# Gate operands turned channel-major by DMA transposes, and a second buffer for the output tile

## The chip, the core and the metric

The kernel runs on one core of one Trainium2 chip. The metric is the device time of one execution in microseconds (us); a kernel's figure is the median of its runs. The engines are named as the profile names them: PE (TensorE matmul) and PEld (its weight loads), DVE (VectorE), ACT (ScalarE), POOL (GpSimd), and SP (SyncE), which here only issues DMAs. A trailing q (SPq) is an engine's instruction queue.

## The reference

A gated linear recurrence runs along 5824 positions of 4 sequences, on 256 channels, and its output goes through a multiplicative feed-forward block.

```python
sig_r = 1.0 / (1.0 + np.exp(-r_gate))
sig_i = 1.0 / (1.0 + np.exp(-i_gate))
log_a = c * sig_r * np.log(np.clip(a_base, 1e-06, 1.0 - 1e-06))[None, None, :]   # c = 8
a_t = np.exp(log_a)
norm = np.sqrt(np.maximum(1.0 - a_t * a_t, 1e-06))
x_gated = norm * sig_i * x
for t in range(S):
    h = a_t[:, t] * h + x_gated[:, t]
    y[:, t] = h
...
a = x @ w1          # x: y as 23296 x 256
b = x @ w2          # w1, w2: 256 x 1024
h = a * b @ w3      # w3: 1024 x 1024
return (h @ w_out).astype(np.float32)   # w_out: 1024 x 256
```

## The kernel before

The 23296 tokens are cut into 46 chunks, the first of 256 tokens and the others of 512. Inputs arrive token-major (128 tokens on the partitions, 256 channels in the row). The recurrence needs channels on the partitions, so that DVE's scan can run along the tokens; two operands have to be turned on the way.

For a chunk c the work is this. `load` fetches r, i and x (three DMAs of 512 KB from SP). `tanh_r` and `tanh_i` take the two tanh on ACT (a sigmoid is half of a tanh plus a half), and POOL makes u = sigmoid(i) times x. `tr_r` turns tanh(r) with 8 PE transposes of 128x128 into a PSUM tile `ptr`; `decay` is the exp on ACT that reads `ptr` and writes a. `square` on POOL and `root` on ACT make the norm; `tr_u` turns u into `ptr` too, and `gated` on DVE multiplies norm and u. `scan` (two per chunk) and `cast` on DVE end the recurrence. The feed-forward part takes four quarters per chunk: `up` makes `pa` and `pb` on PE (4 matmuls each), ACT copies `pa` to `sa`, DVE multiplies `sa` and `pb` into `g`; `down` multiplies 128 tokens of g with a weight into `po`. That weight is w3 times w_out, made on the chip once by `fold`. `store` copies half a chunk of `po` (256 tokens) to `ot`, on ACT for the first half and on DVE for the second, and SP writes it out.

PSUM is full: `pa` and `pb` share a pool of three tiles of two banks, `ptr` has one bank (pool `psum_t`), and `po` has one (pool `psum_o`). So the second half's `down` cannot start before the first half's copy has ended, and tr_r and tr_u of all chunks go through one tile.

The order is written out by hand: every engine executes its instructions in the order in which the loop issues them. A step s has four quarters. In step s, PE does `up` of chunk s and `down` of chunk s-2; DVE does gated, scan, scan and cast of chunk s+2, one in each quarter. The gate work of tanh, transposes, exp, square and root is queued in groups of chunks (1, 1, 2, 3, then 4 each), spread over the quarters of the steps before the group's first `gated`, by weights written beside each operation; within a group all roots come last, since tanh and sqrt need different tables on ACT. `load` of a chunk is issued six quarters ahead of its tanh_r. Three buffers each hold r, i, x and `ot`.

Of the kernel before, what the change touches and what calls it, by code (L numbers as in the profile page):

```python
# [18 lines left out]
def kernel(  # L19
# [45 lines left out]
    psum = ctx.enter_context(tc.tile_pool(name="psum", bufs=3, space=bass.MemoryType.PSUM))  # L65
    psum_t = ctx.enter_context(tc.tile_pool(name="psum_t", bufs=1, space=bass.MemoryType.PSUM))
    psum_o = ctx.enter_context(tc.tile_pool(name="psum_o", bufs=1, space=bass.MemoryType.PSUM))

# [24 lines left out]
    def tanh_r(c):  # L93
        n = sizes[c] // P
        t = gates.tile([P, 4, D], BF16, name="th_r", tag="th_r")
        nc.scalar.activation(out=t[:, :n, :], in_=T["r", c][:, :n, :], func=AF.Tanh, scale=0.5)  # L96
        T["thr", c] = t

    def tanh_i(c):
        n = sizes[c] // P  # L100
        t = gates.tile([P, 4, D], F32, name="th_i", tag="th_i")
        nc.scalar.activation(out=t[:, :n, :], in_=T["i", c][:, :n, :], func=AF.Tanh, scale=0.5)  # L102
        u = held.tile([P, 4, D], BF16, name="u_t", tag="u")
        nc.gpsimd.tensor_scalar(t[:, :n, :], t[:, :n, :], 1.0, 0.5, op0=ALU.add, op1=ALU.mult)  # L104
        nc.gpsimd.tensor_mul(out=u[:, :n, :], in0=t[:, :n, :], in1=T["x", c][:, :n, :])  # L105
        T["u", c] = u

    def transposes(src, n):
        pt = psum_t.tile([P, NCB, CT], BF16, name="ptr", tag="ptr")
        for cb in range(NCB):  # L110
            for j in range(n):
                nc.tensor.matmul(  # L112
                    out=pt[:, cb, j * P:(j + 1) * P],
                    lhsT=src[:, j, cb * P:(cb + 1) * P], rhs=ident,
                    is_transpose=True,
                    start=(cb == 0 and j == 0), stop=(cb == NCB - 1 and j == n - 1))
        return pt

    def tr_r(c):
        T["pr", c] = transposes(T["thr", c], sizes[c] // P)  # L120
        T["a", c] = held.tile([P, NCB, CT], F32, name="a_t", tag="a")

# [16 lines left out]
    def tr_u(c):  # L139
        T["pu", c] = transposes(T["u", c], sizes[c] // P)  # L140

# [70 lines left out]
    def fold(mi):  # L212
        w3 = ffn.tile([P, DFF], BF16, name="w3_t", tag="w3")
        nc.gpsimd.dma_start(out=w3, in_=moe_w3[mi * P:(mi + 1) * P, :])
        pt = psum_t.tile([P, KD, P], BF16, name="ptw", tag="ptr")
        for k in range(KD):
# [15 lines left out]
    for k, g in enumerate(groups):  # L232
        last = g[0] - LEAD - 1
        first = groups[k - 1][0] - LEAD if k else last
        ops = []
        for c in g:
            ops.append((1.04, lambda c=c: tanh_r(c)))
            ops.append((1.04, lambda c=c: tanh_i(c)))
            ops.append((0.7, lambda c=c: (tr_r(c), decay(c, 0))))
            ops.append((0.7, lambda c=c: (decay(c, 1), square(c))))  # L240
        for c in g:
            ops.append((1.05, lambda c=c: root(c)))
        total = sum(d for d, _ in ops)
        npos = 4 * (last - first + 1)
        acc = 0.0
        for n_op, (d, fn) in enumerate(ops):
            pos = min(npos - 1, int(npos * (acc + d / 2) / total))
            queue.setdefault((first + pos // 4, pos % 4), []).append(fn)
            if n_op < 4 * len(g) and n_op % 4 == 0:
                tanh_at[g[n_op // 4]] = 4 * first + pos  # L250
            acc += d
# [21 lines left out]
    for s in range(s0, NCH + LAG):  # L273
        for mp in range(4):
# [56 lines left out]
```

## Time and profile before

| | us |
|---|---|
| median of 3 runs | 681.7 (680.56 to 685.91) |
| the profiled execution's own time | 687.18 |
| its span in the trace | 685.4 |
| PE busy | 555.9 (81% of the span) |
| DVE busy | 492.2 (72%) |
| ACT busy | 440.6 (64%) |
| POOL busy | 274.1 (40%) |
| granted TensorE clock, mean | 0.974 of full speed |

The stages differ, so the shares of the whole span say little. Until about 99 us the first chunks go through the gate work, the weights arrive and are folded; from there to about 607 us all parts run side by side, in a pattern that repeats every four steps; then the gate work is done, from about 651 us the recurrence too, and only `up` and `down` are left. The profile is read stage by stage: first the stretches, then who waits for whom in one stretch, then single quarters in order of time.

### The profile page before, as it was taken

Reading aid. Unit: us, or ns where it says so; the run is one execution under the profiler, and the core shown is the slowest. Engines: PE = TensorE matmul, PEld = TensorE weight load, DVE = VectorE, ACT = ScalarE, POOL = GpSimd, SP = SyncE. Lnnn points to the kernel's source line nnn. Section 1 sums busy time; section 2 is a strip of 40 time slices with the busy share of each in tenths; the row PEclk is TensorE's granted clock in tenths of the full one; section 3 lists DMA queues with packets and bytes.
Section 4 is the critical chain, followed back from the end, with each engine's and each line's share of the span. In section 5 each row is a group of like instructions: output and inputs, shape, how many; then the busy total and the mean of one; then the engine's idle time right before and its main releaser. Section 6 shows DMA issues by size and latency. Waiting matters only on the chain.

```text
span 685.4 us, 9681 instructions
## 1 busy us (share of the span) xinstructions
PE 555.9 (81%) x3784; PEld 346.3 (51%) x3784; DVE 492.2 (72%) x438; ACT 440.6 (64%) x492; POOL 274.1 (40%) x155
## 2 busy tenths in 40 slices
PE   0326478788897898898887898898898898899995
PEld 0224344455564455555554555555555555556564
DVE  1316269678787788788787788788688688898851
ACT  6734068586785687687685677687687686574441
POOL 3663238626514516516515435435435433330000
PEclk9999599899999999999998999999999999999999
DMA  9993524282482365355355167168068055111112
GB/s 205 352 249 98 123 62 142 90 270 85 137 260 95 123 198 171 121 188 183 121 176 180 44 194 254 36 195 261 32 189 273 32 178 188 35 47 47 47 62 77
DMA packets 99901, 99.71 MB, mean 145 GB/s; under 512 B 4112, under 2 KB 98320, under 8 KB 99856
## 3 DMA queue, kind: packets, MB, share of 16 engines
q1 hardware_dynamic: 97120, 95.44, 43.7%
q0 software_dynamic: 2736, 3.67, 3.2%
q8 instruction: 29, 0.48, 0.3%
q14 instruction: 16, 0.13, 0.1%
HBM read 78.91 MB, written 23.86 MB: 150 GB/s over the span
## 4 chain that ended last, share of the span: by engine, by line
PE 35%; DVE 23%; issue 18%; ACT 14%; DMA 6%; POOL 3%; SPq 1%; DVEq 0%; ACTq 0%; POOLq 0%
PE po L197 14%; PE pa L178 8%; DVE g_t L190 7%; PE pb L186 7%; ACT sa L181 7%; DVE h_t L164 5%; DMA i_t<-in_i_gate_dram 5%; DVE y_t L170 4%; DVE ot L207 4%; PE ptr L112 4%; PE pw L223 2%; ACT a_t L125 2%; DVE nrm L144 2%; ACT th_i L102 2%; POOL nrm L131 1%
## 5 line engine op out<-in xcount | busy, mean ns | idle before, releaser
L190 DVE TENSOR_TENSOR g_t<-sa,pb 128x1024 bf16<-128x1024 bf16 (+1 forms) x184 | 220.9, 1200 | 111.5 <-ACT sa L181 100.9
L181 ACT CAST sa<-pa 128x1024 bf16<-128x1024 f32 (+1 forms) x184 | 184.2, 1001 | 118.6 <-PE pa L178 116.5
L197 PE MATMUL po<-wp_sb,g_t 128*128 128x256 bf16 x1456 | 189.3, 274 | 53.2 <-DVE ot L207 51.5
L197 PEld LDWEIGHTS <-g_t 128*128 128x128 bf16 x1456 | 142.7, 98 | 115.2 <-issue 66.1
L186 PE MATMUL pb<-y_t,w_sb 128*128 128x512 bf16 (+1 forms) x736 | 190.3, 382 | 2.9 <-ACT sa L181 2.9
L178 PE MATMUL pa<-y_t,w_sb 128*128 128x512 bf16 (+1 forms) x736 | 191.6, 384 | 0.2 <-DVE g_t L190 0.2
L104 POOL TENSOR_SCALAR th_i<-th_i 128x1024 f32<-128x1024 f32 (+1 forms) x46 | 50.7, 1102 | 241.4 <-ACT th_i L102 151.8
L164 DVE TENSOR_TENSOR_SCAN h_t<-a_t,h_t,nrm 128x512 f32<-128x512 f32 (+3 forms) x90 | 137.2, 1526 | 0.0
L131 POOL TENSOR_TENSOR nrm<-a_t 128x1024 f32<-128x1024 f32 (+1 forms) x46 | 99.1, 2153 | 79.8 <-ACT a_t L125 79.8
L105 POOL TENSOR_TENSOR u_t<-th_i,x_t 128x1024 bf16<-128x1024 f32 (+1 forms) x46 | 117.8, 2562 | 5.9 <-DMA x_t<-in_x_dram 2.1
L186 PEld LDWEIGHTS <-w_sb 128*128 128x128 bf16 x736 | 73.1, 99 | 92.0 <-issue 8.9
L125 ACT ACTIVATE a_t<-ptr,la 128x512 f32<-128x512 bf16 (+1 forms) x92 | 66.7, 772 | 68.4 <-PE ptr L112 68.4
L178 PEld LDWEIGHTS <-w_sb 128*128 128x128 bf16 x736 | 69.9, 99 | 47.5 <-issue 2.7
L144 DVE SCALAR_TENSOR_TENSOR nrm<-nrm,ptr 128x1024 f32<-128x1024 f32 (+1 forms) x46 | 55.6, 1209 | 38.2 <-PE ptr L112 20.3
L136 ACT ACTIVATE nrm<-nrm 128x1024 f32<-128x1024 f32 (+1 forms) x46 | 48.1, 1051 | 9.5 <-POOL nrm L131 9.4
L112 PE MATMUL ptr<-ident,th_r 128*128 128x128 bf16 x364 | 29.7, 228 | 29.8 <-ACT th_r L96 17.7
L170 DVE CAST y_t<-h_t 128x1024 bf16<-128x1024 f32 (+1 forms) x46 | 51.7, 1123 | 0.1
L205 ACT COPY ot<-po 128x512 f32<-128x512 f32 x46 | 27.0, 586 | 37.5 <-PE po L197 37.5
L102 ACT ACTIVATE th_i<-i_t 128x1024 f32<-128x1024 f32 (+1 forms) x46 | 48.4, 1052 | 2.5 <-DMA i_t<-in_i_gate_dram 2.5
L96 ACT ACTIVATE th_r<-r_t 128x1024 bf16<-128x1024 f32 (+1 forms) x46 | 48.7, 1059 | 0.2
L112 PEld LDWEIGHTS <-th_r 128*128 128x128 bf16 x364 | 25.0, 102 | 33.4 <-ACT th_r L96 19.8
L112 PE MATMUL ptr<-ident,u_t 128*128 128x128 bf16 x364 | 30.6, 232 | 11.1 <-POOL u_t L105 10.2
(28 smaller groups left out, 153.0 us busy)
## 6 DMA issues: line engine op xcount, KB each, us to landing
out_dram<-ot SPq DMA_DIRECT2D x91, 256.0 KB, 2.2
r_t<-in_r_gate_dram SPq DMA_DIRECT2D x45, 512.0 KB, 4.5
i_t<-in_i_gate_dram SPq DMA_DIRECT2D x45, 512.0 KB, 5.5
x_t<-in_x_dram SPq DMA_DIRECT2D x45, 512.0 KB, 5.8
w_t<-in_moe_w_dram POOLq DMA_DIRECT2D x8, 256.0 KB, 5.8
w_sb<-in_moe_w_dram POOLq DMA_DIRECT2D x2, 512.0 KB, 8.0
wo_sb<-in_moe_w_out_dram POOLq DMA_DIRECT2D x1, 512.0 KB, 14.3
r_t<-in_r_gate_dram SPq DMA_DIRECT2D x1, 256.0 KB, 2.9
```

Of the source, the lines that this page charges most:

```text
L105: nc.gpsimd.tensor_mul(out=u[:, :n, :], in0=t[:, :n, :], in1=T["x", c][:, :n, :])
L112: nc.tensor.matmul(out=pt[:, cb, j * P:(j + 1) * P], lhsT=src[:, j, cb * P:(cb + 1) * P], rhs=ident, is_transpose=True, start=(cb == 0 and ...
L125: nc.scalar.activation(out=T["a", c][:, cb, :w], in_=T["pr", c][:, cb, :w], func=AF.Exp, scale=la4[:, cb:cb + 1], bias=la4[:, cb:cb + 1])
L131: nc.gpsimd.tensor_mul(out=t[:, :, :w], in0=T["a", c][:, :, :w], in1=T["a", c][:, :, :w])
L144: nc.vector.scalar_tensor_tensor(out=T["n", c][:, :, :w], in0=T["n", c][:, :, :w], scalar=1e-3, in1=T["pu", c][:, :, :w], op0=ALU.max, op1 ...
L164: nc.vector.tensor_tensor_scan(T["h", c][:, cb, lo:hi], T["a", c][:, cb, lo:hi], T["n", c][:, cb, lo:hi], init, ALU.mult, ALU.add)
L170: nc.vector.tensor_copy(out=T["y", c][:, :, :w], in_=T["h", c][:, :, :w])
L178: nc.tensor.matmul(out=pa[:, q, :w], lhsT=w1_sb[:, cb, m * P:(m + 1) * P], rhs=T["y", c][:, cb, :w], start=(cb == 0), stop=(cb == NCB - 1))
L181: nc.scalar.copy(out=sa[:, :, :w], in_=pa[:, :, :w])
L186: nc.tensor.matmul(out=pb[:, q, :w], lhsT=w2_sb[:, cb, m * P:(m + 1) * P], rhs=T["y", c][:, cb, :w], start=(cb == 0), stop=(cb == NCB - 1))
L190: nc.vector.tensor_mul(out=T["g", c][:, 2 * mp:2 * mp + 2, :w], in0=sa[:, :, :w], in1=pb[:, :, :w])
L197: nc.tensor.matmul(out=T["po", c][:, j % 2, :], lhsT=T["g", c][:, k, j * P:(j + 1) * P], rhs=wp_sb[:, k, :], start=(k == 0), stop=(k == KD ...
```

## The change

The pool `psum_t` and the PE transposes are gone; `psum_o` gets two buffers, and the fold's transposes, which used the bank of `ptr`, now use `psum_o` too. tanh(r) and u are written by ACT and POOL with the two halves of the channels apart, each as four blocks of 128x128. A DMA transpose issued from SP turns all eight blocks in one instruction and writes a tile in SBUF (`rt` for tanh(r), `ut` for u); chunk 0 takes two DMAs for each. `decay` and `gated` read these tiles where they read `ptr`. The `rt` DMA is issued right after tanh_r. The exp of a chunk comes after the two tanh of the next chunk of its group, and `tr_u`, now a DMA, moves from the quarter of `gated` to the place just ahead of the exp. The moment of a load still is six quarters ahead of its tanh_r.

```diff
-    psum_t = ctx.enter_context(tc.tile_pool(name="psum_t", bufs=1, space=bass.MemoryType.PSUM))
-    psum_o = ctx.enter_context(tc.tile_pool(name="psum_o", bufs=1, space=bass.MemoryType.PSUM))
+    psum_o = ctx.enter_context(tc.tile_pool(name="psum_o", bufs=2, space=bass.MemoryType.PSUM))
...
     def tanh_r(c):
         n = sizes[c] // P
-        t = gates.tile([P, 4, D], BF16, name="th_r", tag="th_r")
-        nc.scalar.activation(out=t[:, :n, :], in_=T["r", c][:, :n, :], func=AF.Tanh, scale=0.5)
-        T["thr", c] = t
+        t = gates.tile([P, NCB, 4, P], BF16, name="th_r", tag="th_r")
+        nc.scalar.activation(out=t[:, :, :n, :].rearrange("p cb j q -> p j cb q"),
+                             in_=T["r", c][:, :n, :].rearrange("p j (cb q) -> p j cb q", q=P),
+                             func=AF.Tanh, scale=0.5)
+        T["pr", c] = turn(t, n, "rt")
+        T["a", c] = held.tile([P, NCB, CT], F32, name="a_t", tag="a")
...
-        u = held.tile([P, 4, D], BF16, name="u_t", tag="u")
+        u = gates.tile([P, NCB, 4, P], BF16, name="u_t", tag="u")
...
-        nc.gpsimd.tensor_mul(out=u[:, :n, :], in0=t[:, :n, :], in1=T["x", c][:, :n, :])
+        nc.gpsimd.tensor_mul(out=u[:, :, :n, :].rearrange("p cb j q -> p j cb q"),
+                             in0=t[:, :n, :].rearrange("p j (cb q) -> p j cb q", q=P),
+                             in1=T["x", c][:, :n, :].rearrange("p j (cb q) -> p j cb q", q=P))
...
+    def turn(src, n, tag):
+        dst = (gates if tag == "rt" else held).tile([P, NCB, 4, P], BF16, name=tag, tag=tag)
+        if n == 4:
+            nc.sync.dma_start_transpose(out=dst.rearrange("p cb j q -> p (cb j) q"),
+                                        in_=src.rearrange("p cb j q -> p (cb j q)"))
+        else:
+            for cb in range(NCB):
+                nc.sync.dma_start_transpose(out=dst[:, cb, :n, :],
+                                            in_=src[:, cb, :n, :].rearrange("p j q -> p (j q)"))
+        return dst.rearrange("p cb j q -> p cb (j q)")
...
-        T["pu", c] = transposes(T["u", c], sizes[c] // P)
+        T["pu", c] = turn(T["u", c], sizes[c] // P, "ut")
...
-        for c in g:
-            ops.append((1.04, lambda c=c: tanh_r(c)))
-            ops.append((1.04, lambda c=c: tanh_i(c)))
-            ops.append((0.7, lambda c=c: (tr_r(c), decay(c, 0))))
-            ops.append((0.7, lambda c=c: (decay(c, 1), square(c))))
+        for c in g + [None]:
+            if c is not None:
+                ops.append((1.04, lambda c=c: tanh_r(c)))
+                ops.append((1.04, lambda c=c: tanh_i(c)))
+            if c != g[0]:
+                d = g[-1] if c is None else c - 1
+                ops.append((0.7, lambda d=d: (tr_u(d), decay(d, 0))))
+                ops.append((0.7, lambda d=d: (decay(d, 1), square(d))))
...
                 if mp == 0:
-                    tr_u(c)
                     gated(c)
```

How instructions stand now, at three places. First SP in the running stage, where a row is one DMA (r_t, i_t and x_t are loads, ot the output). Before:

```order
L209 DMA out_0_dram<-ot_2507 128x2x256
L88 DMA r_t_2541<-in_r_gate_dram 128x4x256
L88 DMA i_t_2543<-in_i_gate_dram 128x4x256
L88 DMA x_t_2545<-in_x_dram 128x4x256
L209 DMA out_0_dram<-ot_2583 128x2x256
```

and after:

```order
L115 DMA_TRANSPOSE rt_993<-th_r_991 128x8x128
L209 DMA out_0_dram<-ot_1017 128x2x256
L115 DMA_TRANSPOSE rt_1051<-th_r_1049 128x8x128
L87 DMA r_t_1054<-in_r_gate_dram 128x4x256
L87 DMA i_t_1056<-in_i_gate_dram 128x4x256
L87 DMA x_t_1058<-in_x_dram 128x4x256
L115 DMA_TRANSPOSE ut_1087<-u_t_1023 128x8x128
L209 DMA out_0_dram<-ot_1090 128x2x256
```

Two transposes per chunk have come in between the loads and the stores; each waits on SP for the ACT or POOL instruction that writes its source, and the rows below it wait with it.

Second, ACT in the running stage: from a chunk's tanh_r to its exp (`a_t`). `sa` is the copy of `pa`, one in each quarter. Before:

```order
L96 ACTIVATE th_r_1315<-r_t_1107 128x1024
L181 CAST sa_1322<-pa_1317 128x1024
L102 ACTIVATE th_i_1339<-i_t_1109 128x1024
L181 CAST sa_1352<-pa_1347 128x1024
L125 ACTIVATE a_t_1391<-ptr_1382,la4_89 128x512 x2
```

and after, for the chunk whose turned tile is rt_993:

```order
L95 ACTIVATE th_r_991<-r_t_802 128x4x2x128
L181 CAST sa_1001<-pa_996 128x1024
L205 COPY ot_1017<-po_979 128x512
L104 ACTIVATE th_i_1021<-i_t_804 128x1024
L181 CAST sa_1031<-pa_1026 128x1024
L95 ACTIVATE th_r_1049<-r_t_876 128x4x2x128
L181 CAST sa_1065<-pa_1060 128x1024
L104 ACTIVATE th_i_1082<-i_t_878 128x1024
L125 ACTIVATE a_t_995<-rt_993,la4_86 128x512
L181 CAST sa_1098<-pa_1093 128x1024
```

The exp has moved behind the next chunk's two tanh: three copies of `pa` stand between tanh_r and exp where there were two.

Third, SP at the start, from the load of chunk 2 (r_t_112 before, r_t_109 after). Before, the next rows are the loads of chunk 3:

```order
L88 DMA r_t_112<-in_r_gate_dram 128x4x256
L88 DMA i_t_114<-in_i_gate_dram 128x4x256
L88 DMA x_t_116<-in_x_dram 128x4x256
L88 DMA r_t_140<-in_r_gate_dram 128x4x256
L88 DMA i_t_142<-in_i_gate_dram 128x4x256
```

and after:

```order
L87 DMA r_t_109<-in_r_gate_dram 128x4x256
L87 DMA i_t_111<-in_i_gate_dram 128x4x256
L87 DMA x_t_113<-in_x_dram 128x4x256
L119 DMA_TRANSPOSE rt_121<-th_r_119 128x2x128 x2
L119 DMA_TRANSPOSE ut_130<-u_t_127 128x2x128 x2
L87 DMA r_t_138<-in_r_gate_dram 128x4x256
L87 DMA i_t_140<-in_i_gate_dram 128x4x256
L87 DMA x_t_142<-in_x_dram 128x4x256
L115 DMA_TRANSPOSE rt_149<-th_r_147 128x8x128
L115 DMA_TRANSPOSE ut_159<-u_t_155 128x8x128
```

Chunk 0's transposes stand behind the loads of chunks 0, 1 and 2, and chunk 1's behind those of chunk 3.

## Rows read from the trace of the kernel before

**Rows 1.** Page, engines: busy us, share of the span, instructions.
```profile
PE 555.9 (81%) x3784; PEld 346.3 (51%) x3784; DVE 492.2 (72%) x438; ACT 440.6 (64%) x492; POOL 274.1 (40%) x155
```

**Rows 2.** Stretches of the span, busy us (instructions), clock, DMA share, GB/s.
```profile
core 0: us, PE busy (x) PEld busy (x) DVE busy (x) ACT busy (x) POOL busy (x), PEclk, DMA share, GB/s
0.00:32.00 32.00, 5.00 (x39) 3.69 (x40) 7.89 (x11) 21.83 (x25) 14.46 (x17) 1.00 1.04 273
...
279.03:330.92 51.89, 45.97 (x320) 28.65 (x320) 42.05 (x37) 37.72 (x42) 23.57 (x13) 1.00 0.50 163
330.92:387.35 56.43, 48.80 (x320) 29.78 (x320) 43.81 (x38) 37.71 (x42) 23.05 (x13) 0.94 0.46 150
```

**Rows 3.** PE in order of time, one batch each: start us, us.
```profile
99.28 1.04 PE L197 MATMUL po<-wp_sb,g_t 128*128 128x256 bf16 x8
...
606.80 1.03 PE L197 MATMUL po<-wp_sb,g_t 128*128 128x256 bf16 x8 [1.05 <-DVE ot L207]
...
640.98 0.61 PE L112 MATMUL ptr<-ident,u_t 128*128 128x128 bf16 x8
641.42 1.03 PE L178 MATMUL pa<-y_t,w_sb 128*128 128x512 bf16 x4
...
653.80 1.04 PE L197 MATMUL po<-wp_sb,g_t 128*128 128x256 bf16 x8
...
656.40 1.04 PE L197 MATMUL po<-wp_sb,g_t 128*128 128x256 bf16 x8
```

**Rows 4.** Groups of 99.28 to 606.8 us: busy, mean ns, idle before.
```profile
L197 PE MATMUL po<-wp_sb,g_t 128*128 128x256 bf16 x1200 | 156.8, 274 | 48.4 <-DVE ot L207 48.4
```

**Rows 5.** Waits of 279 to 331 us: total us, times, longest.
```profile
DVE g_t L190 <- ACT sa L181: 8.1, 8, 3.1
...
ACT a_t L125 <- PE ptr L112: 5.9, 3, 4.1
...
PE po L197 <- DVE ot L207: 4.6, 4, 1.7
...
PE ptr L112 <- DVE nrm L144: 1.3, 1, 1.3
```

**Rows 6.** Groups of 279.03 to 330.92 us: busy, mean ns, idle before.
```profile
L190 DVE TENSOR_TENSOR g_t<-sa,pb 128x1024 bf16<-128x1024 bf16 x16 | 19.4, 1210 | 8.1 <-ACT sa L181 8.1
...
L144 DVE SCALAR_TENSOR_TENSOR nrm<-nrm,ptr 128x1024 f32<-128x1024 f32 x5 | 6.1, 1222 | 2.2 <-PE ptr L112 2.2
```

**Rows 7.** Page, DMA: packets, MB, share; issues: KB each, us to landing.
```profile
q1 hardware_dynamic: 97120, 95.44, 43.7%
...
out_dram<-ot SPq DMA_DIRECT2D x91, 256.0 KB, 2.2
...
x_t<-in_x_dram SPq DMA_DIRECT2D x45, 512.0 KB, 5.8
```

**Rows 8.** All engines in order of time, start of the span.
```profile
9.00 1.00 ACT L125 ACTIVATE a_t<-ptr,la 128x256 f32<-128x256 bf16 x2
...
11.95 3.90 SPq L88 DMA_DIRECT2D x_t<-in_x_dram  x1
...
16.16 1.06 ACT L96 ACTIVATE th_r<-r_t 128x1024 bf16<-128x1024 f32 x1
...
17.82 1.06 ACT L102 ACTIVATE th_i<-i_t 128x1024 f32<-128x1024 f32 x1 [0.60 <-DMA i_t<-in_i_gate_dram]
...
30.04 2.66 POOL L105 TENSOR_TENSOR u_t<-th_i,x_t 128x1024 bf16<-128x1024 f32 x1
...
39.88 1.06 ACT L136 ACTIVATE nrm<-nrm 128x1024 f32<-128x1024 f32 x1 [3.68 <-POOL nrm L131]
40.84 0.57 ACT L181 CAST sa<-pa 128x512 bf16<-128x512 f32 x1
```

**Rows 9.** The wait list of SP's own queue, whole span.
```profile
SPq L209 <- DVE ot L207: 243.3, 45, 8.0
...
SPq L88 <- POOL u_t L105: 44.4, 14, 3.8
```

More of the change, by code (lines that the diff above doesn't have):

```diff
@@ L102, in tanh_i @@
         nc.scalar.activation(out=t[:, :n, :], in_=T["i", c][:, :n, :], func=AF.Tanh, scale=0.5)
-        u = held.tile([P, 4, D], BF16, name="u_t", tag="u")
+        u = gates.tile([P, NCB, 4, P], BF16, name="u_t", tag="u")
         nc.gpsimd.tensor_scalar(t[:, :n, :], t[:, :n, :], 1.0, 0.5, op0=ALU.add, op1=ALU.mult)
-        nc.gpsimd.tensor_mul(out=u[:, :n, :], in0=t[:, :n, :], in1=T["x", c][:, :n, :])
+        nc.gpsimd.tensor_mul(out=u[:, :, :n, :].rearrange("p cb j q -> p j cb q"),
+                             in0=t[:, :n, :].rearrange("p j (cb q) -> p j cb q", q=P),
+                             in1=T["x", c][:, :n, :].rearrange("p j (cb q) -> p j cb q", q=P))
         T["u", c] = u
[L108 to L121, printed above, removed]
+    def turn(src, n, tag):
[8 more added lines that the diff above has]
+        return dst.rearrange("p cb j q -> p cb (j q)")
     def decay(c, cb):
@@ L214, in fold @@
         nc.gpsimd.dma_start(out=w3, in_=moe_w3[mi * P:(mi + 1) * P, :])
-        pt = psum_t.tile([P, KD, P], BF16, name="ptw", tag="ptr")
+        pt = psum_o.tile([P, KD, P], BF16, name="ptw", tag="po")
         for k in range(KD):
@@ L248 @@
             queue.setdefault((first + pos // 4, pos % 4), []).append(fn)
-            if n_op < 4 * len(g) and n_op % 4 == 0:
-                tanh_at[g[n_op // 4]] = 4 * first + pos
+            if n_op == 0:
+                tanh_at[g[0]] = 4 * first + pos
+            elif n_op < 4 * len(g) - 2 and n_op % 4 == 2:
+                tanh_at[g[n_op // 4 + 1]] = 4 * first + pos
             acc += d
```

## The prediction

> **What bounds the kernel now.** I start with the busy times [rows 1] and keep only that PE is the fullest engine and DVE the next: the span has stages, so I go on by stretches [rows 2]. The stretch from 279.03 to 330.92 us is four steps of the running stage; it repeats, but for three disturbed places such as the next stretch of 56.43 us. In it PE is busy 45.97 of 51.89 us at full clock, DVE 42.05, ACT 37.72, POOL 23.57, and the DMA engines 0.50. So no transfer limits it, and a step takes 12.97 us.
>
> How long the stage is comes from PE in order of time [rows 3]: the first `down` is at 99.28 us, and the one at 606.80 us is the last that I count. Between them are 1200 `down` matmuls [rows 4], 16 of chunk 0 and 37 times 32, so 38 steps in 507.5 us, 13.36 each with the disturbed places in.
>
> What a step could take shows at the end, where only `up` and `down` are left: one `down` starts 2.60 us after the other (653.80, 656.40), [rows 3], so four quarters are 10.4 us and four steps 41.6. The running stage takes 10.3 us more per four steps. Eight batches of PE transposes explain 3.5 to 4.9 of them (a batch occupies PE for 0.44 us, 640.98 to 641.42, or 0.61 by its duration, [rows 3]); PE's wait for the DVE copy of `ot`, which is the wait for the one `po` tile, 4.6; and PE's wait for the one `ptr` tile 1.3 [rows 5]. These add up to 9.4 to 10.8: PE, with its waits, is the bound, and the change takes away all three.
>
> **The change, part by part.**
>
> *PE.* 728 transposes and as many weight loads go. `down` of the second half no longer waits for the first half's copy. PE would then need 41.6 us per four steps.
>
> *What is next.* DVE is busy 42.05 us in the same four steps [rows 2], just above PE's 41.6. DVE now also idles 8.1 us for `sa` [rows 5, 6]. Part of this is PE being late with `pa`, and part is ACT being held 5.9 us by exps that wait for PE's `ptr` [rows 5]. If all of it goes, a step is 42.05 / 4 = 10.5 us; if all stays, (42.05 + 8.1) / 4 = 12.5 us. Both causes are hit, but three engines with 42, 42 and 38 us of work in fixed order will still trip over each other, so I take the middle, 11.5 us. The gain is 38 x (13.36 - 11.5) = 71 us, with ends of 109 and 33.
>
> *After 607 us.* Four more steps lose one batch each: 4 x 0.44 to 0.61, 2 us.
>
> *Other operands.* `gated` and the exps read SBUF instead of PSUM. `g`, with one operand from SBUF, takes 1210 ns and `gated`, whose other operand is from PSUM too, 1222 [rows 6]: nothing to gain or lose; 0.2 us either way on one `gated` per step would be 8 us, inside the range. The tanh and POOL's u are written in another order. I cost this at nothing, because ACT's 37.72 and POOL's 23.57 us lie beside 46 of the new four steps; ACT would need 8 us more, 2 us on each tanh_r, before that cover is gone.
>
> *The DMAs.* The trace of before shows no DMA transpose. Each moves 256 KB within SBUF. By bytes, the queue's 95.44 MB in 43.7% of 685.4 us [rows 7] give 0.82 us of all 16 engines. By pieces, its 97120 packets give 3.08 ns per packet over 16 engines, and 128 partitions x 8 blocks are 1024 pieces: 3.16 us. The nearest row is the 256 KB store, 2.2 us to landing with all latency [rows 7], so I take about 1 us of the engines and 2 to 3 us to landing. The engines' load per four steps is then 26 + 8 x 1 = 34 us of 46, and even at 3.16 it is 51.3, or 12.8 us a step. The Trainium skill ("DMA: Bandwidth & Descriptors", Latency and other measured facts) gives DMA transposes 261 GB/s when the source is not contiguous: that would be an estimated 1.0 us each, and the sum would stay as it is.
>
> *Waits that are added.* SP waits for tanh_r before each `rt`, and for POOL's u before each `ut`; behind these stand stores and loads. SP already spends 243.3 us waiting for DVE's copies and 44.4 for POOL's u [rows 9], with no engine held by it: loads go out six quarters (over 16 us) ahead and land in 5.8 [rows 7], and stores have three `ot` buffers. The exp now waits for a DMA, but three quarters after its tanh_r, 8.6 us at the new pace, against 2.2 to 5.8 us to landing [rows 7]. Both cost nothing; without that cover it is the second rival.
>
> *The start.* Here it does cost. The last load of chunk 2 leaves SP at 11.95 + 3.90 = 15.85 us, held by the data ahead of it; the DMA engines are full until 32 us at 273 GB/s, and chunk 1's i_t lands only at 17.82 [rows 2, 8]. The two transposes of chunk 0 are issued after that load, behind some 2.1 MB (x of chunk 1, all of chunk 2), so they land near 25 us. Chunk 0's first exp moves from 9.00 [rows 8] to about 25. ACT's order hands most of it on: tanh_r of chunk 1, now 16.16, comes near 30. Later in the start, SP holds the transposes of chunks 2 and 3 behind a load that waits for POOL's u of chunk 2 (6 us after its tanh_r, 30.04 + 2.66), but the waits for data still in flight are gone. I put the first `sa`, now 40.84 [rows 8], near 55: 14 us late, between 8 (the weight folds that follow wait for other things as well) and 22.
>
> *Sum.* -71 - 2 + 14 = -59. The profiled execution took 687.2 us (span 685.4), which gives 628; the median of the runs is 5.5 lower, 681.7, which gives **623 us**. The forecast's own range puts the step between 10.9 and 12.3 us with the start at 8 and 22: 681.7 - 93 - 2 + 8 = 595 to 681.7 - 40 - 2 + 22 = 662.
>
> **Rivals.**
>
> *The engines' queue becomes the bound: slower.* If one transpose holds the DMA engines, or SP in issuing it, for t, a step takes (26 + 8t) / 4. The total is 681.7 + 38 x ((26 + 8t)/4 - 13.36) + 12; at t = 3.16 that is 673, and above t = 3.4 it is over 1% slower; at t = 4 it is 737. For it: no row shows data that changes partitions on the way, and 1024 pieces for 256 KB are four times as many per byte as now. Against it: even the price per piece, 3.16, stays under the point. Chance 0.16. The Trainium skill speaks for this rival ("VectorE: DVE Perf Modes", Rules for kernel authors, with The three transpose paths): a 128x128 transpose belongs on TensorE where PSUM will do, 390 ns against 1309 by DMA. Eight blocks one after another at that figure would be an estimated 10.5 us, a step of 27.5 and a total near 1230. The trace agrees with it so far as PE's eight blocks in 0.61 us [rows 3] are cheap, cheaper than that page has them.
>
> *The exps wait.* `rt` stands on SP behind a store or a load that waits, or in the queue behind a load, and each exp of the stage's 39 chunks holds ACT, then `sa`, `g` and PE. At 1 us each this gives back 39: 662, range 640 to 675. For it: ACT executes in order, and SP is now one line for three kinds of work. Against it: the 8.6 us. Chance 0.17. At 1.5 us each or more, 39 x 1.5 = 59, the gain is all gone and the kernel stays where it was: 682, chance 0.06.
>
> **How the numbers follow.** About 1% either way is what a measurement of this kernel can tell from no change. The forecast has 0.61. Faster by over 1% is forecast and waiting exps, 0.78; the same 0.06; slower 0.16. The predicted time is the likeliest case's, 623. From 590 to 680 the range holds the forecast, the smaller waits and half of the case without change, 0.81.
>
> **What would show it.** Right: no wait of `po` for `ot`; first `sa` near 55 us; four steps in about 46 us with DVE busy over 90%; the exps' wait for `rt` under 6 us per four steps; the DMA share in the stage 0.65 to 0.75. Wrong in the sum: DVE or PE still waiting 8 us per four steps. Wrong in mechanism: transposes that land after more than 8 us, a DMA share near 1, or SP busy issuing.

## The result, and the profile after

The changed kernel takes 627.35 us (median of 4 runs, 623.59 to 630.42) against 683.81 us (4 runs, 680.56 to 686.01): a ratio of 0.9175, interval 0.9107 to 0.9244. The forecast was 623 us, range 590 to 680. The profiled execution took 630.42 us, its span is 628.7 us; that of before took 687.2, so the profiles differ by 56.8 us.

The busy times of the page after, and four steps of the running stage, from one `gated` to the fourth after it (columns as in [rows 2]); they answer to [rows 1, 2]:

```profile
PE 505.0 (80%) x3000; PEld 301.7 (48%) x3056; DVE 518.0 (82%) x438; ACT 441.0 (70%) x492; POOL 296.7 (47%) x155
```

```profile
217.29:262.98 45.69, 42.30 (x251) 25.02 (x256) 45.33 (x37) 38.69 (x44) 26.05 (x13) 1.00 0.92 230
```

Four steps fell from 51.89 to 45.69 us, 11.42 each. PE is not the fullest engine any more: DVE is, busy 45.33 of 45.69 us. But DVE was given nothing to do. Its instructions are the same 37, and yet they take 3.3 us more than in [rows 2]. So the first question about this profile is not what DVE waits for, since it shows hardly a wait, but which of its instructions became longer.

PE in order of time (start us, us), at its first output tile, 1200 `down` matmuls later, and at the end; this answers to [rows 3]:

```profile
117.49 1.04 PE L197 MATMUL po<-wp_sb,g_t 128*128 128x256 bf16 x8
...
556.73 1.04 PE L197 MATMUL po<-wp_sb,g_t 128*128 128x256 bf16 x8
...
613.93 1.04 PE L197 MATMUL po<-wp_sb,g_t 128*128 128x256 bf16 x8
...
616.53 8.02 PE L197 MATMUL po<-wp_sb,g_t 128*128 128x256 bf16 x72
```

The first `down` comes at 117.49 instead of 99.28 us: the start lost 18.2 us. From there to the end of the span it is 511.2 us instead of 586.1: the rest gained 74.9. The 38 steps that the prediction counts, 1200 `down` matmuls from the first one on, take 439.2 us instead of 507.5, 11.56 each with the disturbed places in; what follows them takes 71.9 instead of 78.6. Where only `up` and `down` are left, one `down` follows the other after 2.60 us, as before.

The waits of the whole span (total us, times, longest), beside [rows 5]:

```profile
PE pa L178 <- DVE g_t L190: 31.0, 35, 1.7
...
DVE g_t L190 <- ACT sa L181: 30.1, 24, 14.1
...
ACT a_t L125 <- DMA rt<-th_r: 25.3, 4, 15.1
```

PE's wait of `po` for `ot`, 48.4 us in [rows 4], is not in the list any more. PE now waits for DVE's `g`. The exps wait for a DMA four times in all, and never after 150 us.

The groups with DVE's and POOL's costliest lines, beside [rows 6] (busy us, mean ns). First the scan and the cast before, from 279.03 to 330.92 us:

```profile
L164 DVE TENSOR_TENSOR_SCAN h_t<-a_t,h_t,nrm 128x512 f32<-128x512 f32 x8 | 12.2, 1529 | 0.0
...
L170 DVE CAST y_t<-h_t 128x1024 bf16<-128x1024 f32 x4 | 4.8, 1198 | 0.0
```

and after, from 217.29 to 400 us:

```profile
L190 DVE TENSOR_TENSOR g_t<-sa,pb 128x1024 bf16<-128x1024 bf16 x65 | 78.0, 1200 | 1.4 <-PE po L197 1.1
...
L164 DVE TENSOR_TENSOR_SCAN h_t<-a_t,h_t,nrm 128x512 f32<-128x512 f32 (+1 forms) x32 | 59.7, 1866 | 0.0
...
L107 POOL TENSOR_TENSOR u_t<-th_i,x_t 128x1024 bf16<-128x1024 f32 x16 | 41.3, 2583 | 1.3
...
L170 DVE CAST y_t<-h_t 128x1024 bf16<-128x1024 f32 x16 | 22.4, 1397 | 0.0
...
L144 DVE SCALAR_TENSOR_TENSOR nrm<-nrm,ut 128x1024 f32<-128x1024 f32 x17 | 20.6, 1212 | 0.0
...
L207 DVE COPY ot<-po 128x512 f32<-128x512 f32 x16 | 10.8, 678 | 0.0
```

The scan has gone from a mean of 1529 ns to 1866 (two of the 32 are shorter scans of 128 columns), the cast from 1198 to 1397; `g`, `gated` and the copy of `ot` are what they were. A mean can hide two kinds of instruction, so one looks at single ones. DVE and POOL in order of time, in a step in which POOL works and two steps later, when it doesn't:

```profile
310.93 1.27 DVE L164 TENSOR_TENSOR_SCAN h_t<-a_t,h_t,nrm 128x512 f32<-128x512 f32 x1
311.91 1.13 POOL L106 TENSOR_SCALAR th_i<-th_i 128x1024 f32<-128x1024 f32 x1 [3.15 <-ACT th_i L104]
312.13 1.19 DVE L190 TENSOR_TENSOR g_t<-sa,pb 128x1024 bf16<-128x1024 bf16 x1
313.13 2.36 POOL L107 TENSOR_TENSOR u_t<-th_i,x_t 128x1024 bf16<-128x1024 f32 x1
313.24 3.32 DVE L164 TENSOR_TENSOR_SCAN h_t<-a_t,h_t,nrm 128x512 f32<-128x512 f32 x1
315.44 2.81 POOL L131 TENSOR_TENSOR nrm<-a_t 128x1024 f32<-128x1024 f32 x1
316.49 1.19 DVE L190 TENSOR_TENSOR g_t<-sa,pb 128x1024 bf16<-128x1024 bf16 x1
317.60 1.20 DVE L170 CAST y_t<-h_t 128x1024 bf16<-128x1024 f32 x1
...
333.65 1.27 DVE L164 TENSOR_TENSOR_SCAN h_t<-a_t,h_t,nrm 128x512 f32<-128x512 f32 x1
...
338.26 0.68 DVE L170 CAST y_t<-h_t 128x1024 bf16<-128x1024 f32 x1
```

A scan takes 1.27 us and a cast 0.68 when POOL stands. The scan at 313.24 starts while POOL computes u, and ends at 316.56, 1.07 us after u's end at 315.49. The cast at 317.60 ends at 318.80, 0.55 us after the square's end at 318.25. Both look as if DVE waited for POOL's instruction to end, inside its own busy time. In the means this is (1.866 - 1.27) x 8 + (1.397 - 0.68) x 4 = 7.6 us per four steps, against 4.1 before, by the same sum. `g` at 312.13 lies beside POOL's work and is not longer; one of its operands is in PSUM.

The DMA rows of the page and of the issues (as in [rows 7]):

```profile
q1 hardware_dynamic: 193312, 119.30, 73.1%
...
rt<-th_r SPq DMA_TRANSPOSE x47, 3.4
ut<-u_t SPq DMA_TRANSPOSE x47, 4.4
```

The queue's packets took 0.731 x 628.7 = 459.6 us of 16 engines, 160 us more than before; over 92 turned operands (two for each of 46 chunks, the first of them half as large) that is 1.74 us each. They are 96,192 packets more, or some 1045 per transpose, near the 1024 pieces that the forecast counted. The DMA share of the stage is 0.92.

### The profile page after: what moved, and what is told of

It reads as the page before. It is cut to its first block, busy times and chain, and to the rows that moved or that the text cites. A ratio compares the mean times of both kernels' runs of the same rounds, so it can differ in the third digit from the quotient of the medians.

```text
span 628.7 us, 8281 instructions
## 1 busy us (share of the span) xinstructions
PE 505.0 (80%) x3000; PEld 301.7 (48%) x3056; DVE 518.0 (82%) x438; ACT 441.0 (70%) x492; POOL 296.7 (47%) x155
## 4 chain that ended last, share of the span: by engine, by line
PE 42%; DVE 22%; issue 14%; DMA 9%; SPq 5%; ACT 3%; POOL 3%; DVEq 0%; POOLq 0%; ACTq 0%
PE pa L178 14%; PE po L197 13%; PE pb L186 13%; DVE g_t L190 9%; DVE y_t L170 5%; DMA i_t<-in_i_gate_dram 4%; DVE h_t L164 3%; SPq L87 3%; DVE nrm L144 2%; DVE ot L207 2%; DMA rt<-th_r 2%; DMA w_t<-in_moe_w_dram 2%; SPq L115 1%; POOL u_t L107 1%; DMA r_t<-in_r_gate_dram 1%
## 5 line engine op out<-in xcount | busy, mean ns | idle before, releaser
L178 PE MATMUL pa<-y_t,w_sb 128*128 128x512 bf16 (+1 forms) x707 | 185.5, 380 | 64.3 <-DVE g_t L190 31.0
L106 POOL TENSOR_SCALAR th_i<-th_i 128x1024 f32<-128x1024 f32 (+1 forms) x46 | 64.7, 1406 | 217.9 <-ACT th_i L104 204.0
L164 DVE TENSOR_TENSOR_SCAN h_t<-a_t,h_t,nrm 128x512 f32<-128x512 f32 (+3 forms) x90 | 161.1, 1791 | 0.0
L131 POOL TENSOR_TENSOR nrm<-a_t 128x1024 f32<-128x1024 f32 (+1 forms) x46 | 111.4, 2431 | 30.2 <-ACT a_t L125 30.2
L125 ACT ACTIVATE a_t<-rt,la 128x512 f32<-128x512 bf16 (+1 forms) x92 | 70.7, 806 | 25.3 <-DMA rt<-th_r 25.3
L144 DVE SCALAR_TENSOR_TENSOR nrm<-nrm,ut 128x1024 f32<-128x1024 f32 (+1 forms) x46 | 59.4, 1291 | 29.8 <-ACT nrm L136 29.8
L170 DVE CAST y_t<-h_t 128x1024 bf16<-128x1024 f32 (+1 forms) x46 | 59.7, 1299 | 0.1
L217 PE MATMUL ptw<-ident,w_t 128*128 128x128 bf16 x64 | 7.5, 289 | 43.3 <-DMA w_t<-in_moe_w_dram 43.3
L207 DVE COPY ot<-po 128x512 f32<-128x512 f32 x45 | 30.6, 679 | 5.2 <-PE po L197 5.2
L217 PEld LDWEIGHTS <-w_t 128*128 128x128 bf16 x64 | 6.4, 135 | 45.1 <-DMA w_t<-in_moe_w_dram 44.2
```

The costliest lines, as they stand in the source:

```text
L125: nc.scalar.activation(out=T["a", c][:, cb, :w], in_=T["pr", c][:, cb, :w], func=AF.Exp, scale=la4[:, cb:cb + 1], bias=la4[:, cb:cb + 1])
L131: nc.gpsimd.tensor_mul(out=t[:, :, :w], in0=T["a", c][:, :, :w], in1=T["a", c][:, :, :w])
L144: nc.vector.scalar_tensor_tensor(out=T["n", c][:, :, :w], in0=T["n", c][:, :, :w], scalar=1e-3, in1=T["pu", c][:, :, :w], op0=ALU.max, op1 ...
L164: nc.vector.tensor_tensor_scan(T["h", c][:, cb, lo:hi], T["a", c][:, cb, lo:hi], T["n", c][:, cb, lo:hi], init, ALU.mult, ALU.add)
L170: nc.vector.tensor_copy(out=T["y", c][:, :, :w], in_=T["h", c][:, :, :w])
L178: nc.tensor.matmul(out=pa[:, q, :w], lhsT=w1_sb[:, cb, m * P:(m + 1) * P], rhs=T["y", c][:, cb, :w], start=(cb == 0), stop=(cb == NCB - 1))
```

## The experiments

Each is timed against the kernel before on the same chip; "four steps" are from one `gated` to the fourth after it in the profile of that kernel. The edits are against the changed kernel unless said otherwise.

**e1_one_po: the DMA transposes alone.**

```
-    psum_o = ctx.enter_context(tc.tile_pool(name="psum_o", bufs=2, ...))
+    psum_o = ctx.enter_context(tc.tile_pool(name="psum_o", bufs=1, ...))
```

> The changed kernel with one buffer for po, so the DMA transposes alone. Theory (DVE bounds the loop, and PE may only stay ahead of it because po has two tiles): DVE copies the second half of po behind the cast at the end of a step, PE stands until then, and DVE then runs out of pb; some 1.2 us a step come back, 38 x 1.2 = 45 us, so about 670 us, with PE's wait of po for ot back at 4 us or more per four steps. Rival (DVE is so full that PE's waits are hidden and the second buffer is worth nothing): 625 to 632 us.

Measured: 705.78 us, ratio 1.0312 (1.0269 to 1.0355): slower than the kernel before, which neither theory had. A stretch of four steps, and the wait list of the whole span:

```profile
228.87:282.90 54.03, 45.61 (x260) 26.08 (x259) 44.58 (x38) 37.59 (x42) 24.56 (x13) 0.94 0.71 194
```

```profile
PE po L197 <- DVE ot L207: 80.3, 39, 4.2
```

With the transposes off PE, PE waits for the one output tile longer than before, 80.3 us in the whole span where it was 51.5, and its granted clock falls to 0.94, which no stretch of the two-tile kernel's stage shows. The 38 steps take 511.0 us, against 507.5 before the change; what makes the kernel slower than before is mostly its start, with the first `down` at 114.39 us instead of 99.28. So removing 728 matmuls from the fullest engine gained nothing by itself; the second output tile is worth 705.8 - 627.4 = 78 us to this kernel.

**e8_shared: the other part as far as it goes without the first.** Against the kernel before: its transposes stay on TensorE, and their tile (and the fold's, by the same edit) and the output tile take turns in a pool of two.

```
-    psum_t = ctx.enter_context(tc.tile_pool(name="psum_t", bufs=1, ...))
-    psum_o = ctx.enter_context(tc.tile_pool(name="psum_o", bufs=1, ...))
+    psum_o = ctx.enter_context(tc.tile_pool(name="psum_o", bufs=2, ...))
...
-        pt = psum_t.tile([P, NCB, CT], BF16, name="ptr", tag="ptr")
+        pt = psum_o.tile([P, NCB, CT], BF16, name="ptr", tag="po")
```

> The kernel before, transposes kept on TensorE, with one pool of two tiles through which the output tile and the transposes' tile take turns, so that the output tile can have a second buffer without DMA transposes. Theory (nearly all of the gain is the second output tile): po's wait of 4.6 us per four steps shrinks, but a transposes' tile that is read late (by exp, by nrm) holds up the next output tile, so part of the wait comes back as a wait of po for a_t or nrm; PE still carries 4.8 us of transposes per four steps, 49 to 51 us for four steps: 650 to 675 us. Rival (the gain needs PE free of the transposes): 680 to 700 us.

Measured: 659.65 us, ratio 0.9628 (0.9583 to 0.9674), as the theory had it; four steps take 50.06 us (231.39 to 281.45). From the waits of the whole span:

```profile
PE ptr L111 <- DVE ot L206: 15.7, 12, 2.6
PE ptr L111 <- DVE nrm L143: 15.1, 10, 1.7
...
PE po L196 <- DVE ot L206: 14.0, 9, 1.6
```

The wait for `ot` has shrunk and partly moved to the transposes, which now wait for the tile. Some 25 of the change's 56 us were to be had without a DMA transpose; the rest came only with both parts together.

**e2_no_pool: POOL's arithmetic left out**, to see what DVE's instructions cost without it. u is the tanh of the gate alone, and the root is taken of 1 - a.

```
-        nc.gpsimd.tensor_scalar(t[:, :n, :], t[:, :n, :], 1.0, 0.5, ...)
-        nc.gpsimd.tensor_mul(out=u[...], in0=t[...], in1=T["x", c][...])
+        nc.scalar.activation(out=u[...], in_=T["i", c][...], func=AF.Tanh, scale=0.5)
...
-        nc.gpsimd.tensor_mul(out=t[:, :, :w], in0=T["a", c][...], in1=T["a", c][...])
```

> The changed kernel with all of POOL's arithmetic left out: u is tanh(i) alone, without the sigmoid's scaling and without x, and the norm is made from a and not from a squared. ACT, PE, DVE, the DMAs and the transposes are the same in number. Theory (scan and cast on DVE take 1.85 and 1.37 us on average where 1.27 and 0.68 are seen beside an idle POOL, because they are held while a POOL instruction runs): scan back at about 1.28 us and cast at 0.69, DVE's work per four steps 45.5 - 7.4 = 38 us, below PE's 41.6, so a step of about 10.5 us and some 590 us. Rival (they are longer because of the DMA traffic, or because DVE reads tiles that DMAs write): scan stays near 1.8, cast near 1.3, time 620 to 627.

Measured: 570.66 us, ratio 0.8355 (0.829 to 0.842). Four steps, and the groups of the same stretch:

```profile
290.88:332.48 41.60, 41.60 (x258) 25.05 (x257) 37.74 (x40) 37.36 (x43) 0.00 (x0) 1.00 0.97 252
```

```profile
L140 DVE SCALAR_TENSOR_TENSOR nrm<-nrm,ut 128x1024 f32<-128x1024 f32 x5 | 6.1, 1217 | 0.0
...
L166 DVE CAST y_t<-h_t 128x1024 bf16<-128x1024 f32 x4 | 2.7, 686 | 0.0
```

PE is busy 41.60 of 41.60 us: it is the bound again, at 10.4 us a step. DVE's own work is 37.74 us; the other 45.33 - 37.74 = 7.6 us of the changed kernel are POOL's doing, and this agrees with the sum over the long scans and casts. The DMA share is 0.97 here, so the transfers lengthen nothing on DVE. The total came out below the 590 expected: the stage gives (45.69 - 41.60) / 4 x 38 = 39 us, and the first `down` comes at 95.70, 22 us earlier than in the changed kernel. The start's gain lies between the first `sa` and the first `down`, 36.9 us here and 61.5 in the changed kernel. There PE waits 43.3 us for the slabs of the third weight, whose loads stand on POOL behind its arithmetic (the first is issued at 54.98); in e2 the loads are early, and its wait list has no such row.

**e7_sq_act: only the squares off POOL.**

```
-        nc.gpsimd.tensor_mul(out=t[:, :, :w], in0=T["a", c][...], in1=T["a", c][...])
+        nc.scalar.activation(out=t[:, :, :w], in_=T["a", c][...], func=AF.Square)
```

> The changed kernel with a squared on ACT (1.06 us each, activation Square) instead of on POOL (2.43 us each), nothing else. Theory (DVE is the bound, and its scans and casts are held while POOL works): POOL's 26 us per four steps fall to 16, the held time of DVE falls from 7.4 to some 4.6 us, four steps from 45.7 to 43 us, where PE (42.3) and ACT (38 + 4.2) stand too; 38 steps x 0.67 = -25 us, 600 to 610 us, scan mean 1.6 and cast mean 1.1 us. Rival (DVE's longer scans are waits of another kind, and ACT's added 1.06 us per step comes on the way to sa): 640 to 665 us, scan mean unchanged at 1.85.

Measured: 627.45 us, ratio 0.9158 (0.9119 to 0.9197): no change against 627.35, which falls between the two expectations. Four steps:

```profile
290.76:337.15 46.39, 42.32 (x253) 24.99 (x257) 45.01 (x37) 41.48 (x47) 15.91 (x8) 1.00 0.86 226
```

POOL's 26 us are down to 15.9, yet DVE still takes 45.01, that is 7.3 us over its own work. So the held time does not go by how much POOL works. POOL and DVE in order of time:

```profile
300.07 2.35 POOL L107 TENSOR_TENSOR u_t<-th_i,x_t 128x1024 bf16<-128x1024 f32 x1
```

```profile
300.19 2.79 DVE L170 CAST y_t<-h_t 128x1024 bf16<-128x1024 f32 x1
```

The cast started 0.12 us after u did and ended 0.56 us after u's end. It looks as if what counts is which instruction of DVE meets which of POOL's, and how long POOL's still runs. Why so many meet in each order of the work, and why more after the change than before it, was not tried.

**e9_split2 and e10_split4: the same work of POOL in shorter instructions.** The first halves the two products; the second quarters them and the step between tanh and product.

```
-        nc.gpsimd.tensor_mul(out=u[...], in0=t[...], in1=T["x", c][...])
+        for cb in range(NCB):
+            nc.gpsimd.tensor_mul(out=u[:, cb, :n, :], in0=t[:, :n, cb * P:(cb + 1) * P],
+                                 in1=T["x", c][:, :n, cb * P:(cb + 1) * P])
...
+        for cb in range(NCB):
+            nc.gpsimd.tensor_mul(out=t[:, cb, :w], in0=T["a", c][:, cb, :w], in1=T["a", c][:, cb, :w])
```

> The changed kernel with POOL's two products (u and the square of a) each in two instructions of 512 columns instead of one of 1024; nothing else. Theory (of a DVE instruction that reads two tiles of SBUF, or casts, and a POOL instruction that reads SBUF, one waits until the other instruction has ended; in the trace of the changed kernel every long scan or cast ends about its own duration after a POOL instruction's end): a hold is then 1.2 us at most instead of 2.3, the held time of 8.3 us per four steps falls to 4 to 5.5 us, the step from 11.4 to 10.6 to 10.9 us, and the kernel to 600 to 615 us. Rival (what lengthens DVE goes by POOL's total work, which stays): scan and cast means unchanged at 1.87 and 1.40 us, 622 to 632 us.

> As e9_split2, with four instructions of 256 columns for each of POOL's three steps (the product u, the square, and the +1 and half of th_i). Theory: a hold is 0.6 us at most; scan mean near 1.5 us, four steps 42 to 43 us, where PE's own work of 42.3 us stands: 590 to 608 us. Rivals: unchanged at 622 to 632 us, if holds go by POOL's total; or slower than e9_split2, if DVE and POOL then take turns piece by piece and each scan meets more pieces.

Measured: e9 609.23 us, ratio 0.8915 (0.8862 to 0.8968); e10 615.89 us, ratio 0.9018 (0.8965 to 0.9072). Four steps of e9, and its groups of 250 to 400 us:

```profile
246.88:289.78 42.90, 41.84 (x253) 25.04 (x256) 42.65 (x37) 37.71 (x43) 30.46 (x20) 1.00 0.93 244
```

```profile
L166 DVE TENSOR_TENSOR_SCAN h_t<-a_t,h_t,nrm 128x512 f32<-128x512 f32 (+1 forms) x28 | 47.0, 1678 | 0.0
...
L146 DVE SCALAR_TENSOR_TENSOR nrm<-nrm,ut 128x1024 f32<-128x1024 f32 x14 | 20.2, 1443 | 0.0
L172 DVE CAST y_t<-h_t 128x1024 bf16<-128x1024 f32 x14 | 13.6, 971 | 0.0
```

DVE is down to 42.65 us, 4.9 over its own work, as expected, and a step takes 10.7 us. No work was taken away: cutting two instructions in halves gained 18 us. `gated` is now held too (1443 ns), which it was not where POOL's long instructions happened to miss it.

Four pieces are worse than two: the theory (590 to 608 us) missed, and the second rival has it. The scans are nearly free (1332 ns mean), but now POOL is late. Four steps of e10, a group and the waits of 250 to 400 us:

```profile
247.26:291.50 44.24, 41.67 (x252) 24.99 (x256) 39.96 (x37) 37.20 (x43) 37.45 (x48) 1.00 0.86 230
```

```profile
L109 POOL TENSOR_TENSOR u_t<-th_i,x_t 128x256 bf16<-128x256 f32 x56 | 60.3, 1106 | 0.0
```

```profile
DVE g_t L194 <- ACT sa L185: 13.3, 11, 3.0
ACT nrm L140 <- POOL nrm L134: 12.1, 6, 3.7
```

POOL's 26 us have become 37.45, the squares are late, ACT's root waits for them, and behind the root stand `sa` and `g`. Two things make POOL longer. The pieces cost more in themselves: the median piece of the product u, of the square and of the step ahead of u takes 0.73, 0.61 and 0.40 us, 27.8 us for the 48 of four steps, where the whole instructions at their shortest take 2.35, 1.90 and 1.05, 21.2 us. That is 6.6 of the 11.4 us. The rest, 4.8 us, is POOL standing longer for DVE: the longest piece of u takes 1.73 us.

**e12_one_po_split2: e1 once more, with POOL's halves of e9** (both edits are above).

> e1_one_po (DMA transposes with one output tile) with POOL's two products in halves, as in e9_split2. Theory (e1 came out slower than the kernel before because the copy of the output tile stands on DVE behind scans and casts that POOL holds, and PE with a single output tile stands for it, up to 3 us at a time): shorter holds take some 4 us of the 8.4 us that PE stands per four steps, and with them the clock dips: 650 to 675 us. Rival (PE stands for po because a single tile can't be copied while it is filled, whatever DVE does): 695 to 706 us.

Measured: 642.04 us, ratio 0.9397 (0.9348 to 0.9447), further down than the theory expected. From the waits of the whole span:

```profile
PE po L199 <- DVE ot L209: 37.1, 39, 2.8
```

As many waits as in e1, 39, fell from 80.3 to 37.1 us. So e1 was slow because DVE's copy of the output tile stood behind held scans and casts. The second tile is then worth 642.0 - 609.2 = 33 us, not 78: more than half of its value in the changed kernel is that it hides POOL's holds from PE.

**e3_ot_act: the second copy of the output tile on ACT** (`store` copies with `nc.scalar.copy` in both halves).

> The changed kernel with the second half's copy of po moved from DVE to ACT. Theory (DVE is the bound of the loop): each step loses DVE's 0.68 us; ACT has 38 of 46 us of work per four steps and takes 0.59 more a step. 38 x 0.6 = 23 us, so about 605 us. Rival (the loop is bound by the fixed order of three nearly full engines, as predicted): no gain, or a loss of some us, since ACT is fuller and its copies of pa come later: 625 to 635.

Measured: 622.71 us, ratio 0.9092 (0.9058 to 0.9126). The total is near the rival's, and the stage decides for it: four steps take 45.66 us, as before the edit. DVE in that stretch, and groups of 223 to 406 us:

```profile
223.69:269.35 45.66, 42.40 (x258) 25.02 (x257) 44.92 (x33) 39.37 (x46) 26.86 (x12) 1.00 0.88 231
```

```profile
L164 DVE TENSOR_TENSOR_SCAN h_t<-a_t,h_t,nrm 128x512 f32<-128x512 f32 (+1 forms) x32 | 63.1, 1972 | 0.0
...
L144 DVE SCALAR_TENSOR_TENSOR nrm<-nrm,ut 128x1024 f32<-128x1024 f32 x16 | 23.9, 1496 | 0.0
```

Four copies, 2.7 us, left DVE, and the holds gave 2.3 of them back: scan and `gated` became longer. Here a DVE that is busy all the time because it is held was not relieved by taking away work that is not held. Of the 7.3 us between the two profiles 4.7 lie ahead of the first `down` (112.83 instead of 117.49), where the edit changes nothing. So the start differs by some 5 us from one execution to another, and the total's gain is not shown to be the edit's.

**e5_two_turns: each DMA transpose issued twice**, the second time into a tile that nobody reads.

> The changed kernel with every DMA transpose issued twice, the second time into a tile that nobody reads. Theory (the transfers are hidden, but near their limit: one transpose is 1.74 us of the 16 DMA engines, read from the changed kernel's q1 row, and four steps of 45.7 us fill 0.90 of them): four steps then need 26 + 16 x 1.74 = 54 us of the DMA engines, 13.5 us a step instead of 11.4; some 38 steps give +79 us, 690 to 715 us. Rival (a transpose costs the DMA engines the about 1 us that the forecast took): 26 + 16 x 1 = 42 us per four steps, still below 45.7, and 625 to 640 us.

Measured: 653.94 us, ratio 0.9519 (0.946 to 0.9577), between the two. Four steps, and the wait list of 250 to 400 us:

```profile
274.51:322.72 48.21, 42.37 (x254) 24.99 (x257) 46.82 (x38) 37.33 (x43) 26.11 (x13) 1.00 1.08 262
```

```profile
ACT a_t L128 <- DMA rt<-th_r: 23.1, 6, 5.4
```

Now the queue is full and the exps wait for it; doubling cost 26.6 us. One of the transposes on SP, in the same stretch:

```profile
299.01 3.93 SPq L118 DMA_TRANSPOSE ut<-u_t  x1
```

In the changed kernel SP needs 1.24 us to issue an `rt` (the median) and 0.4 to 0.5 us for a store or a load. At these prices SP would be issuing for about 29 of the 48.2 us; it is issuing for 45.7. So SP is full too, and its longer issues speak for the queue holding it up rather than for SP as the limit by itself. With the 26 us of the other transfers per four steps, taken from [rows 2], a transpose takes about (48.2 - 26) / 16 = 1.4 us of the engines when they are full. The 1.74 of the page is higher, and the DMA share of 1.08 shows that packet times can add up to more than the engines' time; by it I expected too much.

**e6_old_order: a chunk's exps right behind its own tanhs**, as in the kernel before.

```
-        for c in g + [None]:
+        for c in g:
...
-                ops.append((0.7, lambda d=d: (tr_u(d), decay(d, 0))))
+            ops.append((0.7, lambda c=c: (tr_u(c), decay(c, 0))))
```

> The changed kernel with the order of the chunk's own steps as before the change: a chunk's exps and the transpose of its u right behind its own two tanhs, not one chunk later. Theory (the DMA transpose's way of 3.4 us to landing is what the later exps are there for): the exp stands two quarters, 5.7 us, behind its tanh_r, and the transfer is in after 1.1 + 3.4 us at the earliest and waits in SP's queue besides; the exps wait for rt 1 to 2 us each first time in a step, and ACT, whose 38 us per four steps leave 7 idle, passes on little of it: 625 to 640 us. Rival (ACT's wait is passed on to sa and g in full): 4 x 2 us per four steps, 38 steps, +70 us, near 700. Second rival (the later exps were not needed): 622 to 630 and no wait of a_t for rt in the running stage.

Measured: 655.03 us, ratio 0.9557 (0.951 to 0.9604), between the expectations. The waits of the whole span, and one of SP's queue:

```profile
ACT a_t L125 <- DMA rt<-th_r: 60.4, 20, 14.7
```

```profile
SPq L115 <- POOL u_t L107: 96.3, 30, 17.3
```

The exps wait for `rt` 60.4 us instead of 25.3, since the exp now stands close behind its tanh_r, and `rt` stands on SP behind `ut` transposes that wait for POOL's u (17.8 us after the change, 96.3 here). The edit moves both, and what each costs was not separated. About 16 of the 28 us are lost in the first seven steps behind the first `down` (100.1 instead of 84.2 us). So without the later place of the exps and of `ut` half of the gain is gone.

**e4_start: chunks 1 and 2 loaded behind chunk 0's transposes.**

```
-    load(1)
     nc.gpsimd.dma_start(out=wo_sb, ...)
-    load(2)
-    nloaded = 3
+    nloaded = 1
```

> The changed kernel with the loads of chunks 1 and 2 no longer issued ahead of chunk 0's transposes on SP (they follow from the same rule as all later loads). Theory (the start is late because chunk 0's transposes stand behind 3 MB of loads): rt of chunk 0 lands at about 10 us where it took until 24.3, the first sa comes at 46 to 50 us where it was 56.0, and the whole time falls by 5 to 10 us: 617 to 622. Rival (the start is bound by the bytes that have to arrive anyway, and the loads that are later now give it back): first sa at 54 to 58 us, time 624 to 630.

Measured: 625.12 us, ratio 0.913 (0.909 to 0.9169). Its runs overlap with those of the changed kernel, so a gain is not shown, though in the profile the first `sa` moved from 56.04 to 53.69 and the first `down` from 117.49 to 110.04; e3, with the old order of loads, has 112.83. Most of the start's loss is not the order of these loads.

**e11_best: e9 with e4, and the eight slabs of the third weight loaded before the first step** into buffers of their own.

```
+            if s == -1:
+                load_w3(2 * mp)
+                load_w3(2 * mp + 1)
             if 0 <= s < NCH:
                 up(s, mp)
```

> e9_split2 together with e4_start (chunks 1 and 2 loaded behind chunk 0's transposes) and with all eight slabs of the third weight loaded two steps earlier (at the step before the first one of the FFN) into eight buffers. Theory (in e9_split2 PE stands 44 us for those slabs between 56 and 125 us, and reaches its first output tile at 118.8 us; before the change at 99.3): they come during the 14 us in which PE waits for the chunks, and the first output tile falls to 98 to 108 us; the running stage stays at 10.7 us a step: 590 to 600 us. Rival (the start is bound by bytes, so that slabs fetched earlier only push the chunks' loads later): 602 to 610 us.

Measured: 591.40 us (6 runs, 588.43 to 594.77), ratio 0.8652 (0.8607 to 0.8698): 36 us below the changed kernel, as expected. The first `down` is at 101.34 us, and a step takes 43.03 / 4 = 10.8.

## Why the prediction was right or wrong

**PE was the bound, and all three of its terms go.** Right as to what went: no `po` wait, no transposes, no `ptr` wait. But the terms were not independent. I had added up transposes (3.5 to 4.9 us) and the `po` wait (4.6) as if each could be had alone. e1 shows that without the second tile the transposes' share comes back as a longer wait, and more; e8 that a second tile, shared with the transposes, gives 25 us without them leaving PE.

**The step of 11.5 us.** The size was right (11.42, and 11.56 with the disturbed places in), the reason wrong, so that it was met is luck. I took the middle between 10.5 and 12.5 because three full engines in a fixed order would "trip over each other". Almost none of DVE's wait for `sa` stayed: 8.1 us per four steps in [rows 5], at most 1.4 in the 183 us of the stage's groups above. And the lower end was not what I took it for: DVE's 42.05 us of [rows 2] held 4.3 us of waiting for POOL (42.05 - 37.74), and the change raised this to 7.6, a term that the forecast didn't have. Without POOL the step is 10.4 us by PE, with it 11.42. The Trainium skill has the rule ("SBUF — State Buffer", Who interferes with whom): DVE and GpSimd share a pair of ports to SBUF; an instruction of DVE that reads two tiles of SBUF, or a cast in a two-port mode, contends with one of GpSimd that reads SBUF, and the one that issues first keeps the pair for the whole instruction. The traces agree in these points: scan, cast and `gated` are held, to about POOL's end (the scan ends 1.07 us and the cast 0.55 us after it); `g` and the copy of `ot`, which read PSUM, are not. In the prediction I read `gated` as "nothing to gain or lose" since `g` costs the same with one operand in SBUF; with both there it became one that can be held: 1212 ns here, 1443 in e9, 1496 in e3.

**The exps don't wait, SP's waits cost nothing.** Right in the stage: the longest wait for `rt` is in the start, and after 150 us there is none. The cover that I named, three quarters, is real: e6 takes it away, together with the later place of `ut`, and loses 28 us.

**The queue.** The nearest row, 1 us of the engines, was too low: about 1.4 by e5, 1.74 by the page, so the share in the stage is 0.92 and not 0.65 to 0.75. The Trainium skill's 261 GB/s ("DMA: Bandwidth & Descriptors", Latency and other measured facts) gave an estimated 1.0 us too; the runs show a higher price. It did not matter here, since the point from which the rival decides, 3.4 us, was far off, and eight blocks landed 3.4 to 4.4 us after their issue, not after the 10.5 us that the rival names. In e9 and e2 the share is 0.93 and 0.97, and e2 still ran at PE's own pace; whether the queue is what comes next was not tried.

**The start.** Forecast 14 us late at the first `sa` (55 us), measured 15.2 (56.04). The transposes of chunk 0 left SP behind the load of chunk 2 as forecast, and the first exp ran at 24.32 instead of 25. But the loss grew to 18.2 us at the first `down`, since the folds' slabs come after it: POOL issues the first at 54.98 us, and PE waits 43.3 us for them in all. Some 5 us of the 18.2 are within what e3's start differs by. ACT in the start:

```profile
24.32 1.09 ACT L125 ACTIVATE a_t<-rt,la 128x256 f32<-128x256 bf16 x2 [15.07 <-DMA rt<-th_r]
...
56.04 0.57 ACT L181 CAST sa<-pa 128x512 bf16<-128x512 f32 x1
```

**The sum.** Forecast -71 - 2 + 14 = -59; between the profiles it was -68.3 (the 38 steps) - 6.6 (what follows) + 18.2 (the start) = -56.7. The terms are 3, 5 and 4 us off and partly cancel, which is luck too. The 2 us after 607 us counted the transposes alone. In e1 and e12, which have no transposes on PE but one output tile, that part takes 76.9 us, against 71.9 with two: the other 5 us are `po` again, which the forecast left out there.

## What to carry to other kernels

When a change frees the bound engine, read the next engine's busy time instruction by instruction before taking it as a floor: where one line's durations differ by a factor of two at the same shape, look for what another engine does at those moments. Time that DVE is held by POOL counts as busy, was not got back here by taking other work off DVE, and went by the length of POOL's single instructions rather than by their sum; cutting them in two gained 18 us, and cutting them in four only 11, since the small pieces cost POOL more and POOL then stood longer for DVE. And a transfer that replaces engine work must be tried without the buffer that it frees: here one half of the change made the kernel slower, the other gave less than half of the gain.

## What the runs showed of the hardware

- A DVE scan of 128x512 takes 1.27 us alone and 3.32 beside a POOL product of 2.36 us; a cast of 128x1024 takes 0.68 alone and 2.79 beside one of 2.35. They end 1.07 us, and 0.55 to 0.56 us, after POOL's instruction.
- POOL's product of 128x1024 in four pieces took 4 x 1106 = 4.4 us beside DVE's work, against 2.58 in one; by the median piece, 0.73 us, four take 2.9.
- A DMA transpose of 256 KB within SBUF landed 3.4 to 4.4 us after its issue (medians of `rt` and `ut`), and took 1.4 to 1.74 us of the 16 DMA engines and 1.24 us of SP to issue where nothing held it up.
